# Part of the second output projection and its normalisation moved into the second attention, in a four-layer attention/S4D kernel

## The chip, the cores and the metric

One core of a Trainium2 chip runs the whole program. The metric is the device time of one execution in microseconds (us). Before the change three executions took 2688.76, 2690.48 and 2694.98 us; the median is 2690.48 us.

## What is computed

The reference, cut to what matters (L = 2048 rows, D = 640, H = 32 heads of 20, N = 128 states):

```python
x = A_x
x = x + attn(layernorm(x)) @ wo          # block A, 32 heads, softmax over 2048 keys
x = x + s4d(layernorm(x))                # block B, a long convolution by FFT, plus u * D_skip
x = x + attn(layernorm(x)) @ wo          # block A again, same weights
x = x + s4d(layernorm(x))                # block B again
```

The change is in the third line and in the layer normalisation that opens the fourth.

## The kernel before, in words

`seq` (L1382) runs `attention`, `out_proj` and `ssm` twice. The residual `x` stays in SBUF as 16 row tiles `s` of 128 rows (row = 16*p + i, so "row tile" is one i).

**Attention.** Heads go in 8 groups `g` of four; queries in 4 blocks `qb` of 512; keys in 16 tiles `kt` of 128. A *turn* is one (g, qb), 32 turns in all, written as two nested loops (L951, L953). For each key tile, `scores` (L838) is called twice: it issues eight matmuls on TensorE as 64-row by 32-column tiles into one of two score buffers `S` in PSUM, and one exponential of 128x1024 on ScalarE from `S` to `pt`. `values` (L854) multiplies `pt` by V, some key tiles later, into `pa0` and `pa1`, and after the last key tile VectorE copies and adds the two into `oc` (the block's unnormalised output; each head's softmax sum is row 32j+20 of it). The sums are then inverted by a round trip through DRAM on the GpSimd queue: `sums` writes the four rows to `dn`, `load` brings them back as 128x16 (`dr`), VectorE inverts, `back` writes, `spread` reads them broadcast into `db`, `scale` multiplies `oc` by `db` at the end of the following turn, `store` writes `oc` to the DRAM tensor `ot` (four DMAs). Keys and queries of a turn come by DMAs on the SyncE queue into `kop` and `qop`: `load_k` (L429) for one half of the keys, `load_q` (L438) for one query block; `kop` has one buffer for each half and is reloaded when the group changes, `qop` has two.

**The order of the work** is fixed when the program is built, by a planner (`Plan`, L50): it keeps a clock for TensorE (`plan.pe`), ScalarE and VectorE, adds a cost for each piece emitted (0.22 us for a group of scores, 0.92 for an exponential, 0.865 for a group of values), and in `fill` (L936), after every group of scores, emits what fits. `slot` (L693) emits a step of the projection jobs (queries, keys and values of the later heads) if TensorE's clock plus the step's cost stays 0.5 us ahead of the end of the last planned exponential; `later` is a list of closures with due times. While `plan.keep` is set, each engine's instructions are tied in this order; afterwards the tool chain orders them itself.

**The end.** When the projection jobs of the second attention are done (end of turn (5, 3), the 24th), `end_jobs` (L913) loads `wo` and GpSimd splits it into `woh` and `wol` (a rounded part and the rest, `prefetch`, L993). In the last turn `out_split` (L1015) loads the first 128 columns of `ot` (`otl`) and splits them into `oh` and `ol`. After the attention `out_proj` (L1127) takes the 16 row tiles one by one: 30 matmuls each (5 blocks of 128 of the 640 contracted rows, 3 products, 2 halves of 320 columns), two additions on VectorE into `x`, and for each pair of rows `ln_u` (L1034), which normalises into `uh` and `ul`. `ssm` (L1163) then starts with `stage1`, which reads `uh` and `ul` of all row tiles and the constant `e1s`. `ssm_consts` (L1151) issues the DMAs for its constants.

Of the kernel before, what the change touches and what calls it, by code (L numbers as in the profile page):

```python
# [34 lines left out]
NBLK = len(BLOCKS)  # L35
NEED = (0, 1, 2, 3, 3, 4, 5, 5)
# [25 lines left out]
class Ordered:  # L62


    def __init__(self, engine, plan, tie, count=False):
        self.engine, self.plan, self.tie, self.count, self.last = engine, plan, tie, count, None

    def __getattr__(self, name):
# [4 lines left out]
        def call(out, *a, **k):  # L73
# [11 lines left out]
def mha_s4d_kernel(ctx, tc, x_in, wqkv, wo, lar, aim, cr, ci, ldt, dsk,  # L85
                   c_e1, c_eb, c_f2, c_fa, c_sel, c_lv, c_id, c_sg, c_e16, c_f16, c_id16, out, parts="asas", general=None):
# [48 lines left out]
    with tc.tile_pool(name="op", bufs=1) as op:  # L135
        oneh = op.tile([1, L], F16, name="oneh")
        ge.memset(oneh, 1.0)
        ge.dma_start(onesd, oneh)

# [274 lines left out]
    def attention(x, stats):  # L414
# [4 lines left out]
        for v in Vt:  # L419
            ge.memset(v[:, :, VP * 8:], 0.0)  # L420
            ge.memset(v[:, :, :VP * 8].rearrange("p i (h r) -> p i h r", r=VP)[:, :, :, DH:], 1.0)
        NK = 3 * DH + 1
# [15 lines left out]
        def load_q(g, j, qb):  # L438

            qt = qop[j][qb % 2]  # L440
# [294 lines left out]
        with ExitStack() as c2:  # L735
# [82 lines left out]
            for j in range(2):  # L818
                load_k(0, j, 0)
                load_q(0, j, 0)  # L820
# [15 lines left out]
        ready, scaled = [], []  # L836

        def scores(kt_, kc, qt):  # L838
# [13 lines left out]
            return pt  # L852

        def values(qb, g, kt, pts, pa):  # L854
# [10 lines left out]
            if kt == NI - 1:  # L865
# [9 lines left out]
                if scaled:  # L875
                    scaled.pop()()
# [21 lines left out]
                def scale():  # L898
                    ve.tensor_mul(oc, oc, db[0])
                    later.append((plan.dve + 0.3, store))  # L900
                    later.sort(key=lambda e: e[0])

                def store():
                    for j in range(4):
                        h = 4 * g + j
                        ge.dma_start(ot[h * DH:(h + 1) * DH, 512 * qb:512 * qb + 512], oc[32 * j:32 * j + DH, :])
# [4 lines left out]
                scaled.append(scale)  # L911

        def end_jobs():  # L913
# [5 lines left out]
            if not first_layer:  # L919
# [3 lines left out]
                ve.tensor_max(flag[:, 0:1], flag[:, 0:1], wx[:, 1:2])  # L923
                ve.reciprocal(wx[:, 0:1], wx[:, 1:2])
                ve.tensor_scalar_mul(wx[:, 0:1], wx[:, 0:1], 2.0 ** -4)
                ve.tensor_max(flag[:, 0:1], flag[:, 0:1], wx[:, 0:1])
# [5 lines left out]
            later.extend((plan.pe + 8.0 + 3.0 * n, f) for n, f in enumerate(rest))  # L932
# [14 lines left out]

        last[0] = None
        tail = None
        every = {NBLK - 1, ("v", 3)}  # L950
        for g in range(H // 4):  # L951
            need(NEED[g], ("v", g // 2))
            for qb in range(4):  # L953
                if g == H // 4 - 1 and qb == 3:
                    if tail is None:
                        need(*every)
                        tail = end_jobs()
                    split, fetch = out_split(tail[-1], 1 if first_layer else 2)
                    first = []
                    later.extend(((plan.pe + 7.0, fetch), (plan.pe + 20.0, lambda: first.append(split(0)))))  # L960
                    later.sort(key=lambda e: e[0])
                pa = [pst("A", [P, 512], F32, tag=f"pa{r}", name=f"pa{r}") for r in range(2)]
                for kt in range(NI):
                    kc, pts = P * (kt % 8), []
                    for j in range(2):
                        pts.append(scores(kop[j][kt // 8], kc, qop[j][qb % 2]))
                        if j:
                            ready.append((plan.act, qb, g, kt, pts, pa))
                        fill(j)
                    if kt == 2:  # L970
                        for j in range(2):
# [533 lines left out]
```

## Time and profile before

| | us |
|---|---|
| median of three executions | 2690.48 |
| the profiled execution | 2693.68 |
| its span, first to last instruction | 2691.8 |
| second attention, first to last `oc` copy (32 turns) | 1523.82 to 2462.36 |
| second output projection, starts of its first and last matmul on `po` | 2463.99 to 2534.5 |
| first matmul of the second S4D block (`psx`) to the end of the span | 2534.68 to 2691.8 |

The profile is of one execution. Times in its views are microseconds from the start of the span. A row of the timeline gives start, length, engine, line, operation, output and input, the count of merged instructions, and in brackets how long the engine sat idle before and who ended that. PE is TensorE, PEld its weight loads, ACT ScalarE, DVE VectorE, POOL GpSimd, SPq the SyncE queue that issues DMAs. L77 is a helper's line through which most instructions are recorded, so instructions are told apart by tile names.

### The profile page before, as it was taken

The page shows a single profiled execution, that of the slowest core. Times are in us where ns is not written, and L with a number is a line of the kernel's source. Part 1 is how long each engine was busy: PE and PEld are TensorE (multiplying, and loading weights), DVE is VectorE, ACT ScalarE, POOL GpSimd, SP SyncE. Part 2 cuts the span into 40 slices and gives each one's busy share as a digit, 9 for nine tenths or more (in the row PEclk, how much of TensorE's full clock was granted, in tenths as well). Part 3 has the DMA queues.
Part 4 walks back from the last instruction along what each step waited for, and adds up shares of the span by engine and source line. Part 5 has one row for each costly group of instructions (what it writes and reads, how often), then busy time and mean ns, then how long its engine had stood idle before and what let it go on. Part 6 is the DMA issues. An engine that isn't in the chain of part 4 may idle for free.

```text
span 2691.8 us, 116010 instructions
## 1 busy us (share of the span) xinstructions
PE 2519.0 (94%) x51104; PEld 1432.0 (53%) x51104; DVE 1473.7 (55%) x3295; ACT 2364.3 (88%) x2799; POOL 855.2 (32%) x1283
## 2 busy tenths in 40 slices
PE   7899999999999998899998999999999998888998
PEld 3345444444444443678886444454444443335888
DVE  8687877876856993477776332232232221003865
ACT  7899999999999999676655899999999999996464
POOL 1123323333332334301671122222222223222476
PEclk9999999999999999999999999999999999999999
DMA  6513222322221225354542111111121112112365
GB/s 212 177 49 88 64 77 53 88 58 72 62 54 50 56 66 169 109 229 161 185 146 65 49 52 52 52 56 42 47 63 39 52 39 59 41 37 80 115 189 162
DMA packets 183154, 236.48 MB, mean 88 GB/s; under 512 B 42864, under 2 KB 128368, under 8 KB 180976
## 3 DMA queue, kind: packets, MB, share of 16 engines
q1 hardware_dynamic: 146304, 182.38, 21.2%
q0 software_dynamic: 36336, 46.59, 7.4%
q8 instruction: 403, 6.60, 1.0%
q14 instruction: 111, 0.91, 0.1%
HBM read 152.81 MB, written 76.03 MB: 85 GB/s over the span
## 4 chain that ended last, share of the span: by engine, by line
ACT 50%; PE 27%; issue 9%; DVE 6%; DMA 3%; SPq 1%; POOL 0%; ACTq 0%; DVEq 0%; POOLq 0%
ACT pt L77 49%; PE pa L862 4%; PE psv L1233 3%; PE psy L1243 3%; PE S L845 3%; PE po L1139 2%; PE psx L1221 2%; PE m L598 2%; PE psx L1198 1%; PE po L1133 1%; PE pkf L1113 1%; PE pst L1208 1%; DVE ktab L77 1%; DMA qop<-qs 1%; PE pq L751 1%
## 5 line engine op out<-in xcount | busy, mean ns | idle before, releaser
L77 ACT ACTIVATE pt<-S 128x1024 f32<-128x1024 f32 x2048 | 1921.9, 1037 | 37.5 <-PE S L845 28.4
L862 PE MATMUL pa<-pt,V 64*32 64x512 f32 x16384 | 1102.2, 590 | 1.7 <-DVE oc L77 1.2
L845 PE MATMUL S<-qop,kop 61*32 61x512 f16 x16384 | 883.6, 381 | 114.4 <-ACT pt L77 102.6
L845 PEld LDWEIGHTS <-kop 61*32 61x32 f16 x16384 | 374.0, 89 | 772.3 <-issue 651.4
L862 PEld LDWEIGHTS pa<-pt,V 64*32 64x32 f32 x16384 | 316.9, 106 | 73.4 <-issue 9.1
L77 POOL DMA_DIRECT2D dn<-oc x256 | 126.2, 499 | 709.3 <-DVE oc L77 682.4
L77 DVE TENSOR_SCALAR qc<-m 128x512 f32<-128x512 f32 (+1 forms) x68 | 46.8, 689 | 305.0 <-PE m L598 302.4
L77 DVE COPY oc<-pa 128x512 f32<-128x512 f32 x64 | 44.2, 690 | 305.1 <-PE pa L862 297.4
L77 POOL DMA_DIRECT2D db<-dn x256 | 129.5, 511 | 129.7 <-DMA dn<-dr 126.4
L598 PE MATMUL m<-xh,wh 64*32 64x512 f16 x2560 | 147.9, 379 | 5.0 <-DVE qc L77 5.0
L598 PE MATMUL m<-xh,wl 64*32 64x512 f16 x2560 | 148.7, 377 | 0.0
L598 PE MATMUL m<-xl,wh 64*32 64x512 f16 x2560 | 146.6, 377 | 0.0
L598 PEld LDWEIGHTS <-wh 64*32 64x32 f16 x5120 | 92.8, 93 | 78.0 <-issue 35.7
L77 POOL DMA_DIRECT2D ot<-oc x256 | 130.3, 516 | 3.1 <-DVE oc L77 1.7
L1226 POOL TENSOR_TENSOR t<-t,kb 128x512 f32<-128x512 f32 x80 | 101.9, 1275 | 67.8 <-DVE t L77 66.8
L77 ACT COPY xt<-pst 128x1024 f16<-128x1024 f16 x80 | 81.6, 1023 | 46.7 <-PE pst L1208 46.6
L77 POOL DMA_DIRECT2D dn<-dr x64 | 35.8, 560 | 245.3 <-DVE dr L77 235.5
L77 DVE TENSOR_TENSOR kb<-ktab 128x512 f32<-128x512 f32 x160 | 107.7, 692 | 0.0
L77 DVE TENSOR_SCALAR V<-m 128x160 f32<-128x160 f32 x64 | 20.7, 324 | 157.7 <-PE m L564 157.7
L564 PEld LDWEIGHTS <-xh 128*128 128x128 f16 x960 | 79.7, 98 | 47.0 <-issue 31.6
L1227 POOL TENSOR_TENSOR t<-t,t 128x512 f32<-128x512 f32 x78 | 99.3, 1273 | 8.6 <-DVE t L77 2.6
L320 PEld LDWEIGHTS m<-kb,ka 128*32 128x32 f32 x3840 | 61.0, 109 | 72.0 <-issue 56.1
(281 smaller groups left out, 3970.2 us busy)
## 6 DMA issues: line engine op xcount, KB each, us to landing
ka<-kha SPq DMA_DIRECT2D x80, 256.0 KB
kb<-khb SPq DMA_DIRECT2D x80, 256.0 KB
db<-dn POOLq DMA_DIRECT2D x256, 64.0 KB, 2.5
kpw<-wd POOLq DMA_DIRECT2D x60, 192.0 KB, 5.0
qop<-qs SPq DMA_DIRECT2D x256, 40.0 KB
kop<-ks SPq DMA_DIRECT2D x128, 80.0 KB
ot<-oc POOLq DMA_DIRECT2D x256, 40.0 KB, 2.7
otl<-ot SPq DMA_DIRECT2D x32, 320.0 KB
```

The lines of the kernel that those rows point to most:

```text
L77: made = f(out, *a, **k)
L320: chain(te.matmul(ps[32 * j:32 * j + 32, c8, :], a[n][:, ch, :], b[n][:, dd, :], start=(n == 0), stop=(n == 2), tile_position=(0, 32 * j)))
L564: chain(te.matmul(ps[:, :n], a_[:, ct, sl], m[:, ct, :], start=(k == 0), stop=(k == 14)))
L598: chain(te.matmul(ps[r][32 * t:32 * t + 32, :], a_[rows, ct, 32 * u:32 * u + 32], m[rows, ct, 512 * v:512 * v + 512], start=(k == 0), stop ...
L845: chain(te.matmul(S[32 * t:32 * t + 32, 512 * r:512 * r + 512], kt_[rows, kc + 32 * t:kc + 32 * t + 32], qt[rows, :], start=True, stop=Tru ...
L862: chain(te.matmul(pa[r][32 * j:32 * j + 32, :], V[rows, kt, VP * h:VP * h + 32], pts[j // 2][rows, 512 * (j % 2):512 * (j % 2) + 512], sta ...
L1139: te.matmul(pos[hf], oh[:, ct, :], m[:, ct, 320 * hf:320 * hf + 320], start=False, stop=(ct == NCT - 1 and m is wol))
L1221: te.matmul(px, f2[:, f, :], xt[:, k, :], start=(n == 0), stop=(n == 2))
L1226: ge.tensor_mul(t2, t2, kb)
L1227: (ge if g0 else ve).tensor_add(t1, t1, t2)
L1233: te.matmul(pv[:, g].rearrange("p r i c -> p (r i c)"), t1[:, g * P:g * P + P], fa, start=True, stop=True)
L1243: te.matmul(py[:, i, :], eb[:, 4 * i4 + i, r, :], v[:, r, 4 * i4 + i].rearrange("p g c -> p (g c)"), start=(r == 0), stop=(r == 1))
```

## The change

1. **Order of turns.** In the second attention the last eight turns, (6,0)…(6,3), (7,0)…(7,3), become (6,0), (7,0), (6,1), (7,1), … The group changes at each of these turns, and `kop` is reloaded each time.
2. **Rows inside the attention.** From the turn after `end_jobs`, a generator `rows_out` takes the place of the projection jobs: after a delay of 30 us on the planner's clock it takes one *item* at a time, a row tile with contracted blocks 0 to 2 (groups 0 to 4, complete by then) or 3 to 4 (once both blocks of groups 6 and 7 for its rows are stored), in steps of four matmuls with a planned cost of 0.25 + 4 x 0.147 us; VectorE splits `otl` and adds `po` to `x`. When both items of a row tile are done it is normalised at once, the inverse root by three Newton steps on VectorE.
3. **wo** is split by VectorE instead of GpSimd, with due times, and in two buffers.
4. **Scaling** of the blocks of groups 6 and 7 is due 27 us after the block instead of at the end of the next turn. For the very last block (`at_once`) the sums are spread by a matmul with a constant 0/1 matrix `dsel`, inverted on 128x512 and multiplied, without the round trip.
5. **What is left** goes to `out_proj`: the items not yet done, their halves merged where neither is done; normalisation runs one item later; `u` is computed on ScalarE in this layer too; the S4D constants are asked for from row tile 10 on; ScalarE's later work is tied behind the last exponential (`floor`).

```diff
+            elif self.floor is not None:
+                self.tie(made, self.floor)
...
+        def at_once(oc, blk):
+            pb = pst("M", [P, 512], F32, tag="m0", name="m0")
+            db = ev.tile([P, 512], F32, bufs=1, name="db")
+            te.matmul(pb, dsel[0], oc, start=True, stop=True)
+            ve.tensor_scalar_max(db, pb, 1e-30)
+            ve.reciprocal(db, db)
+            ve.tensor_mul(oc, oc, db)
+            store_block(oc, blk)
...
+                if dsel and blk == NBK - 1:
+                    later.append((plan.dve, lambda: at_once(oc, blk)))
+                    return
...
+                if first_layer or g < H // 4 - 2:
+                    scaled.append(scale)
+                else:
+                    later.append((plan.dve + 27.0, scale))
...
+            def load(self, item):
+                s, c0, c1 = item
+                o = self.w2.tile([P, NCT, P], F32, name="otl")
+                sy.dma_start(o[:, c0:c1], ot[c0 * P:c1 * P, s * P:s * P + P].rearrange("(t p) c -> p t c", p=P))
+                self.loaded.append((item, o))
...
+            def pick(self):
+                for c in (3, 0):
+                    for item in self.left:
+                        s, c0, c1 = item
+                        if c0 == c and (c == 0 or all(4 * g + s // 4 in stored for g in (H // 4 - 2, H // 4 - 1))):
+                            self.left.remove(item)
+                            return item
...
+        def rows_out(rows, x, woh, wol):
...
+            t, done, parts_done = plan.pe + 30.0, [], set()
+            while rows.left or rows.loaded:
+                yield t, 0.0, False, ()
+                if stop:
+                    return
+                if not rows.loaded:
+                    t = ask() - (0.0 if rows.loaded else 4.0)
+                    continue
+                (s, c0, c1), oh, ol = rows.split(ve.tensor_copy)
+                t0, t = plan.dve + 0.2, ask()
+                mm = [(hf, a, m, ct) for hf in range(2) for ct in range(c0, c1) for a, m in ((ol, woh), (oh, woh), (oh, wol))]
+                half, k, pos = len(mm) // 2, 0, [None, None]
+                while k < len(mm):
+                    part_ = mm[k:k + 4]
+                    cost = 0.25 + 0.147 * len(part_)
+                    yield t0, cost, k > 0, tuple(hf for hf in range(2) if k <= half * hf < k + 4)
+                    plan.on_pe(cost)
...
+                if s in parts_done:
+                    stats_of(x, s, rows.mv[:, s, :])
+                    rows.whole.add(s)
+                    normalise(rows, x, s)
+                parts_done.add(s)
...
+        turns = [(g, qb) for g in range(NG) for qb in range(4)]
+        if not first_layer:
+            turns[-8:] = [(g, qb) for qb in range(4) for g in (NG - 2, NG - 1)]
...
+                else:
+                    todo[0], head[0] = rows_out(rows, tail[0], tail[2], tail[3]), None
...
+                if kt == 8 and g2 != g:
+                    need(NEED[g2])
+                    for j in range(2):
+                        load_k(g2, j, 0)
+                        load_q(g2, j, qb2, n + 1)
...
+        if not first_layer:
+            stop.append(True)
+            first = []
...
-                ge.tensor_copy(woh[:, ct, :], wt)
-                ge.tensor_sub(wol[:, ct, :], wt, woh[:, ct, :])
...
+        def halves(ct):
+            wt = staged.pop(0)
+            ve.tensor_copy(woh[:, ct, :], wt)
+            ve.tensor_sub(wol[:, ct, :], wt, woh[:, ct, :])
+            if ct + 2 < NCT:
+                weights(ct + 2)
...
+        def feed():
+            while len(first) < 2 and (rows.left or rows.loaded):
+                if rows.loaded:
+                    first.append(rows.split(se.copy))
+                if rows.left:
+                    rows.load(rows.left.pop(0))
```

More of the change, by code (lines that the diff above doesn't have):

```diff
@@ L35 @@
 NBLK = len(BLOCKS)
+NBK = 4 * H // 4
 NEED = (0, 1, 2, 3, 3, 4, 5, 5)
@@ L138, in mha_s4d_kernel, with stats_of @@
         ge.dma_start(onesd, oneh)
+    def stats_of(x, s, mv):
+        st = sm.tile([P, 2, 6], F32, name="st1")
+        for h in range(2):
+            ve.bn_stats(st[:, h, :], x[:, s, h * 320:h * 320 + 320])
+        ve.bn_aggr(mv, st)
     def ln_stats(get, n):
@@ L948, in attention @@
         last[0] = None
[L949 removed]
+        tail, rows, stop = None, None, []
         every = {NBLK - 1, ("v", 3)}
[L951 to L982 removed]
@@ L983, in attention @@
         for r_ in ready:
             values(*r_[1:])
+        if not first_layer:
+            stop.append(True)
+            first = []
+            while head[0] is not None and head[0][1]:
+                slot()
+            for s in range(NI):
+                two = [(s, 0, 3), (s, 3, NCT)]
+                if set(two) <= set(rows.left):
+                    rows.left = [e for e in rows.left if e not in two] + [(s, 0, NCT)]
         drain_later(True)
-        scaled.pop()()
-        drain_later(True)
+        while scaled:
+            scaled.pop(0)()
+            drain_later(True)
@@ L988, in attention @@
         plan.keep = False
-        first.append(split(1))
+        se.floor = None if first_layer else se.last
         c.close()
-        return *tail[:-1], split, first
+        return *tail[:-1], rows, first
     def prefetch(x, rest):
```

268 lines of the change are left out of this document (189 added, 79 removed).

## The prediction, made before the run

> **What bounds the kernel now.** I read the granted clock first, then the chain that ended last, then the second attention turn by turn, then the projection behind it.
>
> ```profile
> core 0: 2691.8 us, clock 0.996
> ```
>
> No throttle, so TensorE's times compare. The chain by engines:
>
> ```profile
> ACT 50%; PE 27%; issue 9%; DVE 6%; DMA 3%; SPq 1%; POOL 0%; ACTq 0%; DVEq 0%; POOLq 0%
> ```
>
> Half of the end chain is ScalarE, nearly all of it exponentials; a quarter is TensorE. Where each rules is seen in the busy time by windows (columns: length, then busy us of PE, PEld, DVE, ACT, POOL):
>
> ```profile
> 2160.00:2190.00 30.00, 29.25 (x661) 14.29 (x658) 6.39 (x13) 29.58 (x33) 7.11 (x14) 1.00 0.14 33
> 2280.00:2310.00 30.00, 24.43 (x528) 10.22 (x535) 2.41 (x5) 30.00 (x33) 7.10 (x14) 1.00 0.10 26
> 2460.00:2536.00 76.00, 74.36 (x536) 72.14 (x521) 60.33 (x160) 23.86 (x41) 32.08 (x32) 1.00 0.30 91
> ```
>
> While projection jobs run, TensorE and ScalarE are both full. After the jobs ScalarE alone is full, TensorE has room and VectorE works 2.4 of 30 us. In the projection TensorE is full, with VectorE at 60 of 76. The copies of `oc` mark the turns (VectorE, first turn, end of (5,2), then six later ones):
>
> ```profile
> 1523.82 0.69 DVE L77 COPY oc<-pa 128x512 f32<-128x512 f32 x1 [0.70 <-PE pa L862]
> ...
> 2196.29 0.69 DVE L77 COPY oc<-pa 128x512 f32<-128x512 f32 x1 [8.49 <-PE pa L862]
> 2226.10 0.69 DVE L77 COPY oc<-pa 128x512 f32<-128x512 f32 x1 [10.03 <-PE pa L862]
> ...
> 2285.06 0.69 DVE L77 COPY oc<-pa 128x512 f32<-128x512 f32 x1 [19.57 <-PE pa L862]
> 2314.53 0.69 DVE L77 COPY oc<-pa 128x512 f32<-128x512 f32 x1 [20.46 <-PE pa L862]
> 2344.18 0.69 DVE L77 COPY oc<-pa 128x512 f32<-128x512 f32 x1 [20.23 <-PE pa L862]
> ...
> 2462.36 0.69 DVE L77 COPY oc<-pa 128x512 f32<-128x512 f32 x1 [18.52 <-PE pa L862]
> 2463.16 0.69 DVE L77 TENSOR_TENSOR oc<-oc,pa 128x512 f32<-128x512 f32 x1
> ```
>
> An undisturbed turn lasts 2314.53 - 2285.06 = 29.47 us, 0.92 for each of its 32 exponentials; the last eight together 236.26. The 22 turns full of jobs took 672.5 us where 22 x 29.47 = 648.3: even a full TensorE costs only 1.1 us a turn. TensorE within one key tile of a free turn:
>
> ```profile
> 2261.64 0.41 PE L845 MATMUL S<-qop,kop 61*32 61x512 f16 x8 [0.45 <-ACT pt L77]
> 2261.86 1.05 PE L862 MATMUL pa<-pt,V 64*32 64x512 f32 x16
> 2262.72 0.41 PE L845 MATMUL S<-qop,kop 61*32 61x512 f16 x8
> 2263.48 0.41 PE L845 MATMUL S<-qop,kop 61*32 61x512 f16 x8 [0.34 <-ACT pt L77]
> ```
>
> By starts: 0.22 scores, 0.86 values, 0.22 scores, then 0.54 us with nothing issued until the exponential frees a score buffer. The period is 1.84, the gap 8.7 us a turn.
>
> The projection in the end chain, first and last of 16 pairs of rows:
>
> ```profile
> 2463.99 1.71 PE po L1133 x10
> 2465.70 2.93 PE po L1139 x20
> ...
> 2521.63 1.47 PE po L1133 x10
> 2523.10 2.95 PE po L1139 x20
> ```
>
> Ten matmuls take 1.47 and twenty 2.93: 0.147 us each, 4.40 us a row tile, 480 matmuls 70.5 us, back to back.
>
> **The change, part by part.** *Steps that fit.* By the code's constants, `slot` admits a step of 0.25 + 4 x 0.147 = 0.838 when TensorE's clock is at most 2 x 0.92 - 0.5 - 0.838 = 0.50 us past the end of the exponential before last. Score, values and the next score leave it at 0.1 + 0.22 + 0.865 + 0.22 - 0.92 = 0.485, so one step fits; that pushes the next tile to 0.79, none fits; then again: one step for two key tiles, eight a turn. The first comes 30 us in. Over the last eight turns I count 55 steps: six items of blocks 0 to 2 (18 matmuls in five steps), eight of blocks 3 and 4 (12 in three), a third of a ninth: 208 matmuls. Rows 0 to 5 are complete. Removed from behind the attention: 208 x 0.147 = **30.6 us**; 272 matmuls, 40.0 us, remain.
>
> *Steps on TensorE.* Nothing here shows this step between scores; nearest are the value jobs, also on the full array:
>
> ```profile
> 1869.11 0.40 PE L845 MATMUL S<-qop,kop 61*32 61x512 f16 x8
> 1869.44 0.24 PE L564 MATMUL m<-vh,xl 128*128 128x160 f16 x1
> ...
> 1869.87 0.23 PE L564 MATMUL m<-vh,xl 128*128 128x160 f16 x1
> 1870.03 0.41 PE L845 MATMUL S<-qop,kop 61*32 61x512 f16 x8
> ```
>
> Entry: 0.33 less the 0.22 of scores = 0.11. Exit: 0.16 less the 0.07 spacing = 0.09. A step is 4 x 0.147 + 0.20 = 0.79. Two key tiles offer 2 x 0.54 = 1.08. The score behind the step is 0.25 late, and the other buffer's exponential gives it 0.92 - 0.41 = 0.51 of grace. So the steps hide nearly, not surely. The planner's own clock, walked over the eight turns, ends 2.6 us late. From below 0, from above 1.1 a turn as in the full turns, 8 us. I take 2.6.
>
> The Trainium skill, "TensorEngine Tiling (Array Packing)", Key Properties, says that changing the tiling mode drains TensorE, which speaks against cutting the projection into 55 pieces. By that rule each piece pays twice; the trace agrees, with the 0.11 and 0.09 above.
>
> *Order of turns.* Six more changes of group. At one (SyncE):
>
> ```profile
> 2325.78 2.28 SPq L77 DMA_DIRECT2D kop<-ks  x4
> ...
> 2339.32 0.25 SPq L77 DMA_DIRECT2D qop<-qm  x1
> ```
>
> The 20 DMAs hold the queue 13.8 of the 14.7 us that half a turn gives; that turn lasted 2344.18 - 2314.53 = 29.65, 0.18 over. Six times: 1.1. Behind them in the queue stand the new `otl` loads:
>
> ```profile
> L77 SPq DMA_DIRECT2D otl<-ot x32: 359/365/925, 1061.5 to 2519.0; - x32
> 1746.99 4.63 DMA kop<-ks
> 1488.80 1.46 DMA qop<-qm
> ```
>
> Issue is 0.37. Landing isn't shown for them: between the 1.5 and 4.6 that two loads of the chain took, I take 3. An item's load is asked for when the item before it is split: 18 us ahead behind five steps, 11 behind three. Worst, 13.8 + 3 - 11 = 5.8 late, VectorE waits in its split and TensorE behind it. A request in the first 5 of 29.5 us meets this; of nine such items one or two, a few us each, less TensorE's slack: 1.3 (0 to 5). Together the attention grows by **5.0 us** (0 to 12). VectorE's additions there (splits, additions, statistics, Newton steps; in the first turn the halves of `wo`) are some 8 us a turn beside the 27 idle ones; moving `wo` off GpSimd costs nothing under that cover, and a late `oc` copy if it goes.
>
> *Behind the attention.* VectorE becomes the question:
>
> ```profile
> L77 DVE TENSOR_TENSOR x<-x,po 128x320 f32<-128x320 f32 x32 | 15.3, 478 | 5.9 <-PE po L1139 5.9
> L77 DVE BATCH_NORM_STATS2 st<-x 128x6 f32<-128x320 f32 x32 | 15.2, 489 | 0.6
> L77 DVE TENSOR_TENSOR ol<-otl,oh 128x640 fp32r<-128x640 f32 x14 | 12.1, 867 | 0.4
> L77 DVE RECIPROCAL rs<-lt 128x2 f32<-128x2 f32 (+1 forms) x9 | 1.5, 163 | 1.9 <-ACT lt L77 1.9
> L77 DVE RECIPROCAL dr<-dr 128x16 f32<-128x16 f32 x10 | 2.5, 253 | 0.3
> 2482.70 1.36 DVE L77 TENSOR_TENSOR oc<-oc,db 128x512 f32<-128x512 f32 x1
> ```
>
> A whole row tile: 0.87 split + 0.96 additions + 0.98 statistics + about 0.7 small (the aggregate, and six at 0.16 for each pair) = 3.5. A row tile that lacks only blocks 0 to 2: 0.52 + 2.64 = 3.2, while TensorE needs 18 x 0.147 = 2.65 for it. Left are six whole ones, four such, and one item of blocks 3 and 4 (1.3): 35 us. Ahead of them: the `oc` copy and add 1.4, the ninth item's additions 1.0, the rest of row 5's normalisation about 3 (a dozen small ones and the passes over the row), and `at_once`. Its inverse on 128x512 is not in the trace: at least 0.69 as any pass there, and by the two reciprocals (0.253 - 0.163)/14 = 6.4 ns an element, 0.16 + 510 x 0.0064 = 3.4; I take 3.4, with maximum and product 4.8. VectorE: 45 us against TensorE's 40. The first item isn't split beforehand either. In place of the queued-up 70.5 there stand 40.0 + **5.0 us** (1 to 10). The `at_once` matmul (between the 0.41 of a score group, also 512 columns, and four times that) is within that. What `at_once` spares cost nothing before: the last block was scaled 2482.70 - 2463.16 = 19.5 us after its add, with rows 0 to 11 in between. Now rows 12 to 15 are reached near 2464 + 2 + 4 x 2.65 + 2 x 4.4 = 2485. The old way the scaled block would be stored about then and stall them; `at_once` ends near 2473, and the stores land 2.7 later:
>
> ```profile
> ot<-oc POOLq DMA_DIRECT2D x256, 40.0 KB, 2.7
> ```
>
> *Nothing for:* the first layer (same order of work), the S4D constants (asked for at row tile 10, some 25 us ahead of need by the same sum), `u` on ScalarE (23.9 busy of 76).
>
> **Sum**: -30.6 + 5.0 + 5.0 = -20.6. On the profiled execution's 2693.7 (span 2691.8 and 1.9 around it) 2673.1; it stands 3.2 above the median, so on 2690.5 I forecast **2670 us**, by the bounds 2661 to 2682.
>
> **Rivals.** (a) *Slower: the steps stand in front of ScalarE.* If the scores behind a step come too late for the exponential, a step costs ScalarE up to its whole 0.79 plus 0.09 for the longer weight load, 55 x 0.88 = 48 us: -30.6 + 5 + 2.4 + 48 = +25, 2715 us. It decides from (30.6 - 5 - 2.4)/55 = 0.42 us a step on. Against: full turns lost 1.1, not 7 x 0.42 = 2.9. For: these steps' VectorE work gates the next one. This is what the drain rule would give if it were not covered. (b) *Loads behind the key loads.* If three of the nine short items wait the full 5.8, that is 17 instead of 1.3: 2686 us. For: one queue, in order, occupied 13.8 of 29.5 us in each of the last turns. Against: most loads have 18 us. (c) *It doesn't do what it says*: the planner fits only half the steps (items wait for stores that come late), 104 matmuls, 15.3 gained, 7.5 lost: 2683. Against: blocks 0 to 2 need nothing late.
>
> **Chances.** Forecast 0.64, (a) 0.13, (b) 0.15, (c) 0.08. A measurement here tells about 0.2%, 5.4 us, from no change: faster is below 2685.1. (b) falls half on each side of that, (c) mostly below: faster 0.77, within 0.2% 0.10, slower 0.13. The range reaches over (b) and (c) and the low bound: 2659 to 2690.
>
> **What would show it.** Right: about 208 matmuls with `oh` or `ol` before the last exponential, turns of about 30.1 us instead of 29.5, some 45 us from the last `oc` copy to the last `po` instead of 72, and VectorE nearly full in them. Wrong: turns above 32 us with ScalarE idle behind `S` (a); TensorE waiting for `ol` behind `otl` (b); fewer matmuls ahead of the end (c); or a first gap of more than 10 us after the last `pa`.

## The result, and the profile after

The changed kernel takes 2680.59 us (median of five, 2678.44 to 2680.85) where the kernel before took 2692.75 in the executions beside it: a ratio of 0.9955, 95% interval 0.9941 to 0.9970, some 12 us faster. The forecast was 2670 with a range of 2659 to 2690, 20.5 us faster. The time lies in the range; of the gain forecast three fifths came. The profiled execution took 2680.85 us. Its granted clock:

```profile
core 0: 2679.1 us, clock 0.996
```

The chain that ended last, by engines:

```profile
ACT 52%; PE 25%; issue 10%; DVE 6%; DMA 3%; POOL 1%; SPq 0%; ACTq 0%; DVEq 0%; POOLq 0%
```

As before, no throttle over the whole. TensorE's share of the chain fell from 27 to 25%, ScalarE's rose from 50 to 52. The marks of the turns say where that is (VectorE; the end of turn (5,3) and the end of the last turn):

```profile
2226.61 0.69 DVE L78 COPY oc<-pa 128x512 f32<-128x512 f32 x1 [16.40 <-PE pa L892]
...
2472.59 0.69 DVE L78 COPY oc<-pa 128x512 f32<-128x512 f32 x1 [0.40 <-PE pa L892]
```

The last eight turns took 2472.59 - 2226.61 = 245.98 us instead of 236.26. One turn takes from 29.59 to 32.35 us, 30.75 in mean, where 29.47 was undisturbed. The busy time in most of the third of these turns and of the stretch behind the attention (length, then PE, PEld, DVE, ACT, POOL):

```profile
2287.17:2317.50 30.33, 29.14 (x536) 13.19 (x543) 5.17 (x13) 29.80 (x33) 7.10 (x14) 1.00 0.26 70
2472.59:2518.10 45.51, 42.54 (x293) 40.86 (x294) 39.48 (x111) 18.40 (x29) 12.41 (x14) 1.00 0.36 113
```

TensorE is now 96% busy in the turn, and ScalarE, which was full, has 29.80 of 30.33. The profile by pieces, each measured between the same marks in both kernels (`oc` is the VectorE copy, and the last matmul on `po` is read to 0.1 us):

| piece (us) | before | after | difference | forecast |
|---|---|---|---|---|
| start to end of turn (5,3) | 2226.10 | 2226.61 | +0.5 | 0 |
| last eight turns, between `oc` copies | 236.26 | 245.98 | +9.7 | +5.0 |
| last `oc` copy to the last matmul on `po` | 72.14 | 45.51 | -26.6 | -25.6 |
| last matmul on `po` to the end of the span | 157.3 | 161.0 | +3.7 | 0 |
| span | 2691.8 | 2679.1 | -12.7 | -20.6 |

222 matmuls of the projection (on `m`, L1067) ran before `out_proj`, seven whole row tiles and 12 more; 258 stand behind it. Of the 222, 212 ran before the last turn's work ended and ten behind it.

### The profile page after: what moved, and what is told of

It is laid out like the page before. It is cut to its first block, busy times and chain, and to the rows that moved or that the text cites. A ratio compares the mean times of both kernels' runs of the same rounds, so it can differ in the third digit from the quotient of the medians.

```text
span 2679.1 us, 116332 instructions
## 1 busy us (share of the span) xinstructions
PE 2530.0 (94%) x51106; PEld 1425.0 (53%) x51106; DVE 1516.0 (57%) x3451; ACT 2368.7 (88%) x2793; POOL 827.7 (31%) x1256
## 4 chain that ended last, share of the span: by engine, by line
ACT 52%; PE 25%; issue 10%; DVE 6%; DMA 3%; POOL 1%; SPq 0%; ACTq 0%; DVEq 0%; POOLq 0%
ACT pt L78 50%; PE pa L892 4%; PE psv L1419 3%; PE psy L1429 3%; PE S L858 3%; PE psx L1407 2%; PE m L611 1%; PE psx L1384 1%; PE po L1312 1%; DMA kop<-ks 1%; PE pst L1394 1%; PE pkf L1272 1%; DVE ktab L78 1%; PE po L1307 1%; PE pq L764 1%
## 5 line engine op out<-in xcount | busy, mean ns | idle before, releaser
L858 PEld LDWEIGHTS <-kop 61*32 61x32 f16 x16384 | 366.7, 89 | 741.1 <-issue 622.4
```

The costliest lines, as they stand in the source:

```text
L858: chain(te.matmul(S[32 * t:32 * t + 32, 512 * r:512 * r + 512], kt_[rows, kc + 32 * t:kc + 32 * t + 32], qt[rows, :], start=True, stop=Tru ...
```

## The experiments

Code ahead of the end of turn (5,3) is the same in the changed kernel and its twelve variants, and that mark lies anywhere from 2223.4 to 2228.6 us in their profiles. So single profiles are compared by pieces from that mark on. The changed kernel and the seven variants that keep its steps of four have 245.6 to 247.0 us for the eight turns, which tells how far one profile can be trusted. A row's last column is the sum of the three pieces ahead of it; "on `m`" counts matmuls that run ahead of `out_proj`. Kernels without a range were run once.

| kernel | time | on `m` | eight turns | `oc` to last `po` | to the end | sum |
|---|---|---|---|---|---|---|
| before | 2692.75 (2688.76 to 2694.98) | 0 | 236.26 | 72.14 | 157.3 | 465.7 |
| changed | 2680.59 (2678.44 to 2680.85) | 222 | 245.98 | 45.51 | 161.0 | 452.5 |
| e1_order_only | 2700.29 | 0 | 237.34 | 76.42 | 158.3 | 472.1 |
| e3_five | 2683.51 | 240 | 251.48 | 42.63 | 159.0 | 453.1 |
| e2_three | 2681.72 (2680.28 to 2683.60) | 216 | 246.40 | 47.45 | 160.9 | 454.8 |
| e9_three_spaced | 2683.97 (2679.29 to 2688.66) | 168 | 240.70 | 53.50 | 160.4 | 454.6 |
| e13_two_spaced | 2683.91 | 114 | 237.69 | 59.82 | 159.1 | 456.6 |
| e5_norm_late | 2683.80 | 222 | 245.55 | 52.48 | 160.3 | 458.3 |
| e6_round_trip | 2690.40 | 222 | 246.04 | 59.66 | 159.0 | 464.7 |
| e11_ln_exp | 2681.67 (2681.02 to 2684.16) | 222 | 246.25 | 48.38 | 158.7 | 453.3 |
| e12_ln_exp_u | 2683.24 (2678.69 to 2684.55) | 222 | 246.96 | 48.09 | 158.7 | 453.8 |
| e14_row6_late | 2678.59 (2678.09 to 2679.76) | 222 | 246.32 | 45.36 | 160.7 | 452.4 |
| e4_u_dve | 2680.19 (2678.68 to 2683.63) | 222 | 245.96 | 44.97 | 160.1 | 451.0 |
| e8_no_defer | 2683.29 (2680.61 to 2685.60) | 222 | 245.97 | 46.59 | 160.5 | 453.1 |

### The attention: +9.7 us where +5.0 was forecast

Theory A: a step of four is too long for the slack between scores, and ScalarE starts the next exponential late. Rival B: the six more changes of group cost it. Rival C: each step costs a fixed entry and exit, whatever it holds. The first three kernels tell these apart. **e1_order_only** keeps the new order of turns and never starts a step:

```diff
-                    todo[0], head[0] = rows_out(rows, tail[0], tail[2], tail[3]), None
+                    pass
```

> The new order of turns and the one-product inverse stay; no projection row is taken inside the attention, so all 480 matmuls come behind it. Last eight turns by the oc copies: 236.3 us before, 246.0 in the changed kernel. Theory A (each step of four matmuls makes one exponential 0.16 us late, 59 steps, 9.7 us in all; the key reloads cost almost nothing): 236.3 to 237.5 us. Theory B (six more changes of group and loads queued behind key loads): 243 to 246 us. Behind the attention the 16 rows take 70 us of TensorE again, so the whole is about 2 to 5 us slower than before, not faster.

```profile
2226.44 0.69 DVE L78 COPY oc<-pa 128x512 f32<-128x512 f32 x1 [16.41 <-PE pa L892]
...
2463.78 0.68 DVE L78 COPY oc<-pa 128x512 f32<-128x512 f32 x1
```

The eight turns last 237.34 us, 1.1 more than before: within A's range, and B falls. Even of these 1.1 the order of turns has hardly a part. The last copy stands on VectorE behind two splits of whole row tiles, which the changed kernel does not have there:

```profile
2462.30 1.56 DVE L78 TENSOR_TENSOR ol<-otl,oh 128x640 fp32r<-128x640 f32 x2 [18.64 <-ACT oh L78]
```

It starts 3.20 us after the last exponential, where it starts 2.23 us after it in the kernel before and 2.18 in the changed one. The 256 exponentials themselves take 235.85 us from the first start to the last, 235.74 before and 245.52 in the changed kernel. So the order costs 0.1 us and the steps 9.7, and steps are priced by the exponentials from here on. The whole lost more than the 2 to 5 us expected, 6.4 by the sum. **e2_three** and **e3_five** change the size of a step:

```diff
-                    part_ = mm[k:k + 4]
+                    part_ = mm[k:k + 3]
```

> Steps of three matmuls instead of four, with the planner's cost for three (0.25 + 3 x 0.147). Theory A (the score behind the step and the one behind the values that follow are together 2.21 us apart where ScalarE needs 1.84, with about 0.2 us of lead; three matmuls make that 2.06): a step costs ScalarE 0.02 to 0.06, the last eight turns take 238 to 241 us, about the same number of matmuls fits, and the whole is 4 to 8 us faster than the changed kernel (2673 to 2677). Theory C (each change of the array's mode costs ScalarE a fixed amount whatever the length of the step): about 70 to 75 steps at 0.16 us, 248 us or more, and the whole no faster than the changed kernel.

```diff
-                    part_ = mm[k:k + 4]
-                    cost = 0.25 + 0.147 * len(part_)
+                    part_ = mm[k:k + 5]
+                    cost = 0.25 + 0.147 * min(4, len(part_))
```

> Steps of five matmuls while the planner still counts the cost of four, so the rhythm of one step for two key tiles stays. Theory A: 0.31 us a step instead of 0.16, about 55 steps, the last eight turns 251 to 256 us. Theory C: 0.16 a step, 245 to 246 us. More matmuls are done inside (about 250 to 270 of 480).

Copies of `oc`, first of `e3_five`:

```profile
2228.59 0.69 DVE L78 COPY oc<-pa 128x512 f32<-128x512 f32 x1 [16.41 <-PE pa L892]
...
2480.07 0.69 DVE L78 COPY oc<-pa 128x512 f32<-128x512 f32 x1 [0.40 <-PE pa L892]
```

and of `e2_three`:

```profile
2223.75 0.69 DVE L78 COPY oc<-pa 128x512 f32<-128x512 f32 x1 [16.41 <-PE pa L892]
...
2470.15 0.69 DVE L78 COPY oc<-pa 128x512 f32<-128x512 f32 x1 [0.41 <-PE pa L892]
```

Five a step took 251.48 us, as A said; C had it unchanged. (240 matmuls ran inside, fewer than the 250 to 270 expected.) But three a step took 246.40, no less than four: A had forecast 238 to 241, C 248 or more, and both missed, as did the gain of 4 to 8 us. The reason is in the planner: a planned cost of 0.69 instead of 0.84 lets a step stand in consecutive key tiles, 72 steps instead of 59, so the slack has less time to come back. A was then made into an account of the lead that scores have over ScalarE, from TensorE's rows in the changed kernel, one step of four between two scores:

```profile
2291.40 1.05 PE L892 MATMUL pa<-pt,V 64*32 64x512 f32 x16
2292.26 0.41 PE L858 MATMUL S<-qop,kop 61*32 61x512 f16 x8
2292.60 0.42 PE L1067 MATMUL m<-wol,oh 128*128 128x320 f32 x1
2292.86 0.31 PE L1067 MATMUL m<-woh,ol 128*128 128x320 f32 x1
2293.00 0.31 PE L1067 MATMUL m<-woh,oh 128*128 128x320 f32 x1
2293.15 0.31 PE L1067 MATMUL m<-wol,oh 128*128 128x320 f32 x1
2293.39 0.41 PE L858 MATMUL S<-qop,kop 61*32 61x512 f16 x8
2293.61 1.04 PE L892 MATMUL pa<-pt,V 64*32 64x512 f32 x16
2294.47 0.40 PE L858 MATMUL S<-qop,kop 61*32 61x512 f16 x8
```

The scores issue in 0.22, so the step occupies 2293.39 - 2292.48 = 0.91 us: 0.59 for four matmuls and 0.32 for the change (0.12 ahead of the first, 0.11 in the first one's own longer spacing of 0.26, 0.09 behind the last). ScalarE needs a score every 0.92. From the scores behind the step to the next ones TensorE takes 2294.47 - 2293.39 = 1.08, for the values stand in between. A step and the values behind it thus eat 0.91 + 0.22 + 1.08 = 2.21 us where ScalarE grants 1.84, and what lead there is must pay the 0.37; what it can't pay, ScalarE waits. The starts of ScalarE's exponentials in the traces bear this out. Undisturbed they follow each other in 0.90 to 0.92 us. At a step of four (medians) the exponential that the scores behind the step feed starts 0.94 us after the one before it, and the next one, fed by the scores behind the values, 1.08 us later. With five matmuls a step it is 1.14 and 1.08. **e9_three_spaced** and **e13_two_spaced** put three and two matmuls into steps that are planned at the cost of four, so that their rhythm is that of the changed kernel:

```diff
-                    part_ = mm[k:k + 4]
-                    cost = 0.25 + 0.147 * len(part_)
+                    part_ = mm[k:k + 3]
+                    cost = 0.25 + 0.147 * 4
```

> Steps of three matmuls at the planned cost of four, so that there is one step for two key tiles as in the changed kernel. Theory A as refined (a step of n matmuls takes 0.32 + 0.147 n on TensorE; the score after it and the next one, which stands right behind a group of values, share 0.38 + 0.38 us of lead; what a step takes beyond that is ScalarE's loss): three matmuls cost nothing, four 0.15 us, five 0.30. Then the last eight turns fall from 246 to 237.5 to 239.5 us with 160 to 180 matmuls inside instead of 222, the 45 to 60 that are missing stand behind the attention at 0.147 each (6 to 9 us), and the time is that of the changed kernel within 2 us. Rival (each step costs ScalarE about 0.15 us whatever it holds, an entry and exit cost): the last eight turns stay at 244 to 246, and the time is 6 to 9 us longer.

```diff
-                    part_ = mm[k:k + 4]
-                    cost = 0.25 + 0.147 * len(part_)
+                    part_ = mm[k:k + 2]
+                    cost = 0.25 + 0.147 * 4
```

> Steps of two matmuls at the planned cost of four. So far the exponentials lost 0.08 us a step with 3.0 matmuls a step, 0.16 with 3.76 and 0.27 with 4.29: a line through 0 near 2.5 matmuls with a slope of one matmul, 0.147. If that is the law, steps of two are free: the last eight turns take 237.3 to 238.3 us, the 1.1 of the group changes included, with 100 to 125 matmuls inside. Rival (an entry and an exit are paid by each step): 0.05 or more a step, 240 us or more. The time is longer than the changed kernel's by some 6 us either way, since some 100 matmuls more stand behind the attention at 0.147.

Copies of `oc`, of `e9_three_spaced`:

```profile
2223.40 0.69 DVE L78 COPY oc<-pa 128x512 f32<-128x512 f32 x1 [16.41 <-PE pa L892]
...
2464.10 0.69 DVE L78 COPY oc<-pa 128x512 f32<-128x512 f32 x1 [0.40 <-PE pa L892]
```

and of `e13_two_spaced`:

```profile
2225.49 0.69 DVE L78 COPY oc<-pa 128x512 f32<-128x512 f32 x1 [16.41 <-PE pa L892]
...
2463.18 0.69 DVE L78 COPY oc<-pa 128x512 f32<-128x512 f32 x1 [0.40 <-PE pa L892]
```

Steps of two took 237.69 us between the copies, as expected, and are nearly free: the exponentials take 237.23 us, 1.4 more than with the order alone, which is 0.03 for each of the 53 steps that lie in the eight turns. Steps of three took 240.70, 1.2 above the range expected; the exponentials take 240.24, 4.4 us for 53 steps, 0.08 each and not 0. Four cost 9.7 us for 56 steps, six of which hold only two: (9.7 - 0.2)/50 = 0.19 each. Five: 250.98, so 15.1 us, less 0.9 for eight steps of three and eight of two, over 40 steps: 0.36 each. So the third, fourth and fifth matmul of a step cost ScalarE some 0.05, 0.11 and 0.17 us, and behind the attention each costs 0.147 on TensorE. About two and a half matmuls for two key tiles fit under the exponentials; from there on what is moved in is paid nearly in full. That is why 168, 216, 222 and 240 matmuls inside gave sums within 2.3 us of each other. The two spaced kernels missed on the whole, if not by much: by the sum e9 lost 2.1 us to the changed kernel, where at most 2 was expected, and e13 4.1, where some 6 was.

**e5_norm_late** asks whether VectorE's normalisation inside the turns is what delays the steps:

```diff
-                    stats_of(x, s, rows.mv[:, s, :])
-                    rows.whole.add(s)
-                    normalise(rows, x, s)
+                    rows.late.append(s)
...
-        due = []
+        due = [(s, 2) for s in range(0, len(rows.late) - 1, 2)]
```

> The rows that are complete inside the attention get their two additions there but not their statistics and normalisation; those follow behind the attention, two rows at a time. Theory A (a step of four matmuls makes the scores late, whatever VectorE does): the last eight turns stay at 245 to 246.5 us. Rival V (VectorE's normalisation inside the turns delays the steps or the evictions and so ScalarE): they shorten to 241 or less. Behind the attention VectorE gets some 7 rows x 1.7 us = 12 us more. If the part behind the attention is bound by VectorE over most of its length, it grows by 8 to 12 us; if only its first items are, by 0 to 3. No row's normalisation waits for the next item here, so by the deferral theory the stretch from the last matmul on po to the end is 158 to 158.5 us and not 161.

The eight turns stay at 245.55 us, though VectorE's busy time in them falls from 81.4 to 55.8: A holds, V falls. Behind the attention the stretch grows by 7.0 us, between the two ranges expected, and not because VectorE got 12 us more: it is busy 41.0 us there instead of 39.5, since the statistics still ran inside and the passes over the rows went to ScalarE (27.6 us instead of 18.4) and GpSimd (22.9 instead of 12.4). TensorE waits 1.62 and 2.66 us for ScalarE's `uhx` in front of its first S4D matmuls, then 1.85 for `ol`, and has half its clock for 6.8 us from 2483.8 on. The last part of the expectation missed too: the end is 160.3, not 158.

### Behind the attention: at_once and the loads

**e6_round_trip** puts the inversion of the last block back to DRAM:

```diff
-                if dsel and blk == NBK - 1:
+                if dsel and blk == NBK:
```

> Only the last block's inversion is put back to the round trip through DRAM. By the prediction the scaled block is then stored some 15 us later than now, near 2498 us, behind the time at which the rows 12 to 15 are reached, and TensorE stalls: 3 to 6 us from the last oc copy to the last matmul on po. Rival: nothing or up to 2 us faster, because the 4.8 us of maximum, inverse and product on 128x512 leave VectorE at the start of the part behind the attention, which is the stretch where VectorE is the bound.

GpSimd's queue, then TensorE, in this kernel:

```profile
2485.54 0.56 POOL L78 DMA_DIRECT2D dn<-dr  x1 [5.18 <-DVE nb L78]
2493.29 1.41 POOL L1206 TENSOR_TENSOR ulx<-u,uhx 128x640 f16<-128x640 f32 x1 [7.19 <-ACT uhx L78]
2494.66 2.20 POOL L78 DMA_DIRECT2D db<-dn  x4
...
2501.47 2.05 POOL L78 DMA_DIRECT2D ot<-oc  x4 [1.84 <-DVE oc L78]
...
2510.05 1.17 PE L1307 MATMUL po<-woh,ol 128*128 128x320 f32 x3 [14.82 <-DVE ol L78]
```

TensorE stands for 14.8 us and the stretch grows by 14.1, more than twice the upper end of what was expected, since the trip's DMAs (`dn<-dr`, `db<-dn`, the store) share a queue with GpSimd's subtractions for `ulx`, and the store comes only at 2501.47. Some 2 us of the 14.1 are TensorE's clock: behind the stop it has half of it until 2514.4, and its next 16 matmuls take 0.27 us each instead of 0.147. Without `at_once` the changed kernel loses 14.1 of its 26.6 us in this stretch. What `at_once` itself takes of VectorE, in the changed kernel, with TensorE's start and its longest stop:

```profile
2474.53 1.12 PE L878 MATMUL m<-oc,dsel 128*128 128x512 f32 x2 [0.30 <-DVE x L78]
2475.09 1.15 PE L1307 MATMUL po<-woh,ol 128*128 128x320 f32 x4
2478.47 3.35 DVE L78 RECIPROCAL db<-db 128x512 f32<-128x512 f32 x1
2486.74 1.73 PE L1307 MATMUL po<-woh,ol 128*128 128x320 f32 x10 [1.21 <-DVE nr L78]
```

The inverse is 3.35 us; the estimate was 3.4. **e11_ln_exp** takes it off VectorE, and **e12_ln_exp_u** puts `u` back to VectorE besides:

```diff
-            ve.reciprocal(db, db)
+            se.activation(db, db, AF.Ln)
+            se.activation(db, db, AF.Exp, scale=-1.0)
```

> The 128x512 inverse of the last block, 3.35 us on VectorE, is made on ScalarE as exp(-ln) (the last bits of the block differ). Theory: from the last oc copy to the first ten matmuls in one piece at 2486.74 VectorE is the bound, so what is taken from it there shows: the stretch from the last oc copy to the last matmul on po falls from 45.5 to 42 to 43.5 us and the time by 2 to 3 us. Rival: ScalarE's copies into oh come late behind two or three table loads (1.28 us one here) and its two passes, or the block is stored no earlier and the later rows' loads set the start; then less than 1 us, or a loss.

```diff
-            ve.reciprocal(db, db)
+            se.activation(db, db, AF.Ln)
+            se.activation(db, db, AF.Exp, scale=-1.0)
...
-     ln_u(x, i0, m, ln_stats(lambda i: x[:, i0 + i, :], m), uh, ul, up2, not general)
+     ln_u(x, i0, m, ln_stats(lambda i: x[:, i0 + i, :], m), uh, ul, up2, n == 0 and not general)
```

> As the kernel with exp(-ln), and u on VectorE in this layer too as before the change. If the two effects add, the time is that of the exp(-ln) kernel less some 0.5 to 1 us (the stretch from the last matmul on po to the end 160 us and not 161), and it is the fastest of all: 2676 to 2679. Rival: with VectorE relieved at the start u is what it lacks time for; then no difference or a loss of up to 2 us.

ScalarE and TensorE in `e11_ln_exp`:

```profile
2470.99 1.28 ACT L78 ACT_TABLE_LOAD   x1
2476.97 0.63 ACT L78 ACTIVATE db<-db 128x512 f32<-128x512 f32 x1 [4.69 <-DVE db L78]
2477.61 1.28 ACT L78 ACT_TABLE_LOAD   x1
...
2479.44 0.80 ACT L78 CAST oh<-otl 128x256 fp32r<-128x256 f32 x2
2480.80 1.41 PE L1308 MATMUL po<-woh,ol 128*128 128x320 f32 x4 [5.62 <-DVE nr L78]
```

and TensorE's first matmuls behind that wait, with the granted clock behind the POOL column:

```profile
2480.80:2485.00 4.20, 4.20 (x16) 4.20 (x17) 3.75 (x19) 0.51 (x1) 3.97 (x8) 0.50 0.90 293
```

The rival held: the first copies into `oh` stood on ScalarE behind the two passes and the table loads, TensorE's first matmul came at 2480.80, and the stretch grew by 2.9 us. Some 2 us of these are TensorE's clock: behind the wait of 5.62 us TensorE has half its clock, and 16 matmuls take 4.2 us where 2.4 would do. What the exp(-ln) would be worth without that drop was not told apart. `u` on VectorE besides changed nothing more, as its rival had it; the 2676 to 2679 expected were missed.

**e14_row6_late** relieves VectorE another way:

```diff
-                if s in parts_done:
+                if s in parts_done and s < 6:
```

> Row tile 6, whose second item is the last one begun inside the attention, is no longer normalised at once (12 small instructions of the Newton steps, then u, uhx and ulx, some 4 us of VectorE) between the last oc copy and 2493 us, but as a pair with row tile 7. Theory: VectorE is the bound of the first 14 to 27 us behind the attention (13.15 of 14.10 us and 12.55 of 13.30 busy there, 7.83 of 10.00 and 6.31 of 8.50 later), so work moved from the first stretch into the later ones shows: the stretch from the last oc copy to the last matmul on po falls from 45.5 to 42.5 to 44 us and the time by 1.5 to 3, to 2678 to 2679. Rival: what sets that stretch is the chain of single instructions ahead of the first items (the inverse of 3.35 us, then the split), not VectorE's sum; then less than 0.7 us. Or the work comes back at the end: the stretch from the last matmul on po to the end grows by as much.

The stretch stays at 45.36 us, so the theory falls; that the time of 2678.59 lies in the range it gave is luck. The first and second piece behind the last `oc` copy, in the changed kernel:

```profile
2472.60:2486.70 14.10, 11.55 (x84) 10.14 (x84) 13.15 (x28) 2.38 (x4) 3.66 (x8) 1.00 0.71 238
2486.70:2500.00 13.30, 13.26 (x90) 13.26 (x91) 12.55 (x46) 4.98 (x9) 1.82 (x2) 1.00 0.36 104
```

and in this one:

```profile
2470.45:2484.55 14.10, 11.57 (x85) 10.29 (x86) 13.45 (x24) 2.56 (x5) 4.00 (x8) 1.00 0.74 244
2484.55:2497.85 13.30, 13.30 (x92) 13.30 (x93) 10.87 (x32) 6.58 (x10) 2.79 (x2) 1.00 0.26 76
```

In the second VectorE is relieved, 10.87 us busy where the changed kernel has 12.55, and nothing comes of it: TensorE was full there already, with 13.26 of 13.30. In the first VectorE is as full as it was, with TensorE's stops in it. What TensorE waits for at the end of the first piece in this kernel (SyncE's queue, ScalarE, TensorE):

```profile
2473.54 0.36 SPq L78 DMA_DIRECT2D e1s<-in_c_e  x1
2474.34 5.03 SPq L78 DMA_DIRECT2D otl<-ot  x2
2482.76 0.73 ACT L78 CAST oh<-otl 128x640 fp32r<-128x640 f32 x1 [6.95 <-DMA otl<-ot]
2484.40 1.73 PE L1307 MATMUL po<-woh,ol 128*128 128x320 f32 x10 [1.11 <-DVE ol L78]
```

The load of the first whole row tile is asked for behind the S4D constant `e1s`, which is 2048 KB to an `otl`'s 320, and lands 8 us later. In the changed kernel the order is the same (`e1s` at 2475.68, the loads from 2476.16 on, the first S4D matmul waiting for `e1s` until 2484.03). No kernel with `e1s` asked for later was run: that the transfer holds the loads back is read from these rows and not shown by an edit.

### The end: +3.7 us where nothing was forecast

Two causes were suspected: `u` on ScalarE (**e4_u_dve**) and the normalisation that runs one item later (**e8_no_defer**).

```diff
-     ln_u(x, i0, m, ln_stats(lambda i: x[:, i0 + i, :], m), uh, ul, up2, not general)
+     ln_u(x, i0, m, ln_stats(lambda i: x[:, i0 + i, :], m), uh, ul, up2, n == 0 and not general)
```

> In the second layer the normalised row u is computed on VectorE again, as before the change; all else is the changed kernel. Theory D (u on ScalarE puts the square root of the next row behind u and the casts, and costs 3.7 us between the last matmul of the projection and the S4D block): last po to the end of the span 157 to 158 us instead of 161, the whole 2 to 4 us faster than the changed kernel (2677 to 2679). Rival (VectorE is the bound of the projection behind the attention, so 0.6 us more of work for each of nine rows lengthens it): projection 2 to 5 us longer, the whole within 1 us of the changed kernel or slower.

```diff
-            if due and len(whole) == 0:
+            if due:
```

> Behind the attention each row's normalisation runs with its own item and not one item later, as before the change. Deferral theory: the stretch from the last matmul on po to the end falls from 161.0 to 158 to 158.5 us and the time by 2 to 3 us, to some 2678. Rival: the stretch is long because VectorE is behind with its work altogether (it is the bound until the end), then it falls by less than 1 us, or what it gains comes back as a longer way from the last oc copy to the last po (45.5 us now).

The first gives back 0.9 us of the 3.7 and does not lengthen the projection, so it misses its theory and the longer projection of its rival. The second gives back 0.5 and loses 1.1 in the stretch ahead, as its rival had it. Neither is the cause by itself. The changed kernel's rows behind the last matmul on `po` (2518.1):

```profile
2514.97 1.74 ACT L78 ACTIVATE u<-x,nb,rs 128x640 f32<-128x640 f32 x2 [1.55 <-DVE nb L78]
2516.61 1.34 ACT L78 CAST uhx<-u 128x640 f16<-128x640 f32 x2
2517.85 0.20 ACT L78 ACTIVATE lt<-va 128x1 f32<-128x1 f32 x1
2518.08 0.16 DVE L78 RECIPROCAL rs<-lt 128x1 f32<-128x1 f32 x1 [1.41 <-ACT lt L78]
2521.79 0.22 PE L1384 MATMUL psx<-uhx,e1s 128*128 128x128 f16 x1 [3.35 <-DVE x L78]
```

VectorE waits 1.41 us for a root that stands on ScalarE behind `u` and `uhx`, and its last additions into `x` follow late; TensorE's next S4D group waits 3.35 us for the buffers that they free. Before the change TensorE went on at once, with two S4D groups of 12 matmuls that have buffers of their own (`stage1`'s pool X), and then waited only 0.40 us:

```profile
2536.59 0.22 PE L1198 MATMUL psx<-uh,e1s 128*128 128x128 f16 x1 [0.40 <-DVE x L77]
```

Now those groups, whose rows are ready early, were issued from 2484.03 on, in one of the gaps behind the attention. In the four profiles in which none of their matmuls comes before the last one on `po` (before, e1, e11, e12) the end takes 157.3 to 158.7 us; in the ten in which 8 to 24 of them do, 159.0 to 161.0. The end also follows TensorE's first wait in it: 157.3 to 158.7 us where it is 0.24 to 0.59 (before, e1, e11, e12), 159.0 to 159.1 at 1.0 to 1.9 (e3, e13, e6), 160.1 to 161.0 at 2.1 to 3.5 (all others). Half the clock, which TensorE has for 3.4 us in some of these ends (last section), can't be the whole cause: `e9_three_spaced` and `e5_norm_late` take 160.4 and 160.3 us without it. All this is a correlation over kernels which differ in other things too; an edit that holds the two groups back was not run.

No kernel here is shown to be faster than the changed one: `e14_row6_late` has the lowest median (ratio 0.9951, interval 0.9938 to 0.9965), but that interval and the changed kernel's overlap, and its sum from (5,3) on is the same within 0.1 us. By that sum `e4_u_dve` is the lowest, by 1.5, with an interval of 0.9941 to 0.9968.

## Why the prediction had the sign right and the gain too large

By its own terms, forecast against measured:

| step of the prediction | forecast | measured |
|---|---|---|
| matmuls moved ahead of the last `oc` copy | 208 x 0.147 = -30.6 | 212 x 0.147 = -31.2 |
| steps between scores | +2.6 | +9.7 |
| changes of group | +1.1 | +0.1 (`e1_order_only`) |
| loads behind the key loads | +1.3 | at most 0.9, counted in the 9.7 |
| stretch behind the attention over its matmuls | +5.0 | +4.5 (6.1 over 268, less 1.6 over 480 before) |
| "Nothing for" | 0 | +3.7 at the end, +0.5 ahead of (5,3) |
| sum | -20.6 | -12.7 |

**The step that failed** is "Steps on TensorE": "The score behind the step is 0.25 late, and the other buffer's exponential gives it 0.92 - 0.41 = 0.51 of grace. So the steps hide nearly, not surely." Two things were wrong in it. The step was priced at 0.79 from f16 rows; it takes 0.91, and most of the difference is the first matmul, whose weight load of 0.19 us starts only with it, at 2292.60, and which occupies 0.26 instead of 0.147. And the grace was spent once, on the score behind the step; the score after that stands behind a group of values (1.08 us against ScalarE's 0.92) and finds it gone. The bound "from above 1.1 a turn", 8 us, was passed too. Rival (a) had the mechanism, at a price more than four times too high: 0.88 us a step where 0.19 was measured; its turning point of 0.42 a step was never near. The drain rule that was quoted beside it (the Trainium skill, "TensorEngine Tiling (Array Packing)", Key Properties) agrees with the trace in kind: 0.12 and 0.09 of the 0.91 us stand ahead of the step and behind it.

**Right:** the count (208 forecast, 212 measured), the 3.4 us inverse, the "some 45 us" from the last `oc` copy to the last `po`. The changes of group were priced too high, 1.1 for 0.1: the 0.18 us by which one turn was longer was taken for the price of each. Rival (b) did not come. These are all of TensorE's waits for keys and queries in the eight turns of the changed kernel (engine, line, what it waited for: us in all, times, longest):

```profile
PEld L858 <- DMA kop<-ks: 0.9, 3, 0.4
...
PEld L858 <- DMA qop<-qs: 0.4, 1, 0.4
```

Its waits for a late split, the sign that (b) named, add up to 0.9 us in the same list.

**Right in size, in part by luck:** the stretch behind the attention. The prediction made it VectorE's 45 us against TensorE's 40, over the whole stretch. VectorE had 39.5 of 45.5, and TensorE 42.5: to its 268 matmuls of 39.4 us come 1.1 for the two of `at_once` and 1.3 for the two S4D groups, and it stood still for only 3.0. VectorE can have been the bound only in the first 14 us; behind those TensorE was nearly full, and `e14_row6_late` took VectorE's work away without gain. How much of the stops in the first 14 us is VectorE's and how much is the loads' was not told apart. The prediction had put "nothing" for the constants, asked for in good time for their own use; it did not ask which loads stand behind them in the queue. What it said of the round trip, that the stores would "stall them", was right in kind and, at 14.1 us, the part of the change on which the gain behind the attention hangs most.

**Also failed:** "Nothing for: [...] `u` on ScalarE (23.9 busy of 76)". A share of busy time said nothing of what stands in line behind `u` in the last 4 us, and no term asked what TensorE would have left to do while the last additions ran.

## What to carry to other kernels

Filling gaps of a busy engine is free only as long as the lead that its consumer lives on comes back before the next piece: add up the whole period, not the one wait behind the piece, and stop there, because from then on each matmul moved costs nearly what it saves. When work leaves a long queue, look at what the queue had hidden: here a 2 MB load in front of small ones (read from the rows), the last block's DMA trip, 30 us long in `e6_round_trip`, and the last normalisation. And a late engine is seen in what waits behind it in order, not in its share of busy time.

## What the runs showed of the hardware

TensorE's clock fell after the wait at the end. The changed kernel by windows (the number after the POOL column is the granted clock):

```profile
2523.00:2524.00 1.00, 0.79 (x11) 0.62 (x9) 0.64 (x3) 1.00 (x4) 0.47 (x1) 0.53 0.95 311
2524.00:2526.00 2.00, 2.00 (x21) 2.00 (x20) 2.00 (x7) 1.59 (x4) 0.94 (x1) 0.50 0.33 121
2526.00:2527.00 1.00, 1.00 (x17) 1.00 (x15) 0.74 (x4) 0.59 (x1) 0.00 (x0) 0.77 0.00 0
```

About 1.2 us after the 3.35 us wait had ended TensorE worked at half clock for some 3.4 us: its 128x128 matmuls took 0.31 instead of 0.22. The same drop is in `e2_three`, `e4_u_dve`, `e8_no_defer` and `e14_row6_late`, with waits of 3.45, 2.98, 2.11 and 3.15 us, where it begins between 0.4 us before the wait ends and 1.2 after, and not in `e9_three_spaced` and `e5_norm_late` with 2.96 and 2.59. The Trainium skill, "TensorE: Matmul & The Clock Gate", Part 1, has the clock halved after about 3.4 us without work, counted in windows that run freely. The rows agree with the half clock, and the drop lasts about one such window; they show besides that a wait of 2.1 us can bring it and one of 2.96 not.

An inverse of 128x512 on VectorE takes 3.35 us, five times the 0.69 of a copy or a product of that size. Each of the table loads shown on ScalarE, ahead of the logarithm and between it and the exponential, takes 1.28 us, in line with everything else that it does.
